# Attention with expert products on one core: splitting x^T a period earlier, decoding weights with the sign set in the shift, and a reordered fold

## The chip, the cores and the metric

The program runs on 1 core of one Trainium2 chip. The metric is device time in microseconds (us), median of the runs shown. Engines are named as in the profile: PE (TensorE; PEld is its weight loads), DVE (VectorE), ACT (ScalarE), POOL (GpSimd) and SP (SyncE, which issues all transfers).

## What is computed

```python
scores = scale * np.matmul(q, k.transpose(0, 1, 3, 2))      # 8 batches, 8 heads, 576 x 64
kth = np.partition(scores, -top_k, axis=-1)[..., -top_k:-top_k + 1]   # top_k = 32
scores = np.where(scores >= kth, scores, -1000000000.0)
...                                                         # softmax over the kept scores
attn_out = np.matmul(attn, v)
x = attn_out.transpose(0, 2, 1, 3).reshape(B * S, H * D)    # 4608 x 512
a = x @ w1; b = x @ w2                                      # 512 x 1024 each
h = a * b @ w3
out = h @ w_out                                             # 1024 x 512
```

The weights arrive as 64-bit numbers and are made into 32-bit ones on the chip.

## The kernel before, in words

**Slots.** Attention is cut into 144 slots, 18 to a batch (`SLOTS`): a slot is 128 queries for each of two heads. A slot passes through four stages, each in another turn of the loop `for p in range(-1, n_slots + 2)`, so that one turn (called a period here) works on four slots at once: `scores` of slot p+1 (PE, tile `st`, copied by ACT to `s`), `top32_steps` of slot p (DVE), `mask` and `exps` of slot p-1 (ACT, POOL and ACT again, tile `pab`), and `turn`, `values` and `store_x` of slot p-2 (PE tiles `tp` and `ro`, ACT copies `pts`, `pr`, `rec`, DVE writes `xt`, which is x^T).

**The search for the 32nd largest** on DVE opens with a fold of each row's 576 scores into 192 columns, four TENSOR_TENSOR over tile `w` (maximum and minimum of the first two thirds, then the third against that maximum), and goes on with four rounds of MAX8 (tile `top`) with MATCH_REPLACE between them. The first mask on POOL waits for the last operation of the fold that the finder hands out (`folded`).

**Expert products** of a batch are the generator `moe_steps`: one step is one PE matmul, 576 for a batch, and `fill(n)` takes n of them from the queue. `SHARE = 11, 11, 10` gives 32 to a period, so that one batch's products last exactly 18 periods, called a lap here. The steps are, for each half of the 576 rows, 192 matmuls into tiles `ab` (x times w1 and w2), and 96 into `eo`. All weights and x^T are held as a high and a low part. `split_x(h)` makes the parts of x^T, tiles `xf`: four copies on ACT and four subtractions on POOL for each half. Before the change the first `split_x(0)` is the first thing that the generator does when it is first asked for a step, so it stands in the same `fill` as the first `ab` matmuls. The queue gets a batch at the end of the period in which its last slot was stored.

**Weights** come in 80 units (16 of w_out, 48 of w3 and w1 mixed, two to one, 16 of w2). `warm()` starts one unit and moves every unit on its way one step: ACT makes `t` and a part of `y` from the raw `z`, DVE shifts `t` left by 3 into `z`, POOL adds, DVE puts the sign bit on, then ACT and POOL split it (`wh`, `wl`), or PE multiplies w3 by w_out into `pf`, which becomes `wf`. `warm()` is called four times a period, from the first period p = -1 on. Two units share one PSUM tile `t`, from the same three buffers as `pf`.

**Order.** `InOrder` (lines 38 to 53) keeps every engine's instructions in the order in which the program issues them, so that all of them carry line 48 in the profile and are told apart by their tiles. What `moe_steps` hands to `after` (copies out of PSUM, the split) goes on the list `put_off` and is issued at the head of the next `fill`. Places the change touches: `decode` (line 108), `top32_steps` (208), `moe_steps` with its `split_x` (325 to 393), `fill` and `warm` (446 to 475), and the loop (481 to 534).

Of the kernel before, what the change touches and what calls it, by code (L numbers as in the profile page):

```python
# [9 lines left out]
F32 = mybir.dt.float32  # L10
F32R = mybir.dt.float32r
I32 = mybir.dt.int32
# [7 lines left out]
NHP = H // 2  # L20
# [36 lines left out]
def attn_moe(ctx: ExitStack, tc: tile.TileContext, q, k, v, w1, w2, w3, w_out, out, flag, general):  # L57
# [50 lines left out]
    def decode(z, dst=None):  # L108

        if not bank:
            both = ps_m.tile([128, 512], F32, tag="mm", name="t")
            bank.extend((both[:, 256:], both[:, :256]))
        t = bank.pop()
        y = x_p.tile([128, 2 * HS], F32, tag="x", name="y")
        high = z[:, 1:512:2]
        low = z[:, :512].bitcast(U16)[:, 1:1024:4]  # L120
        r = y[:, 256:512].bitcast(I32)
        u = z[:, :256].bitcast(I32)
        act.activation(t, high, AF.Copy, scale=2.0**-112)
        act.activation(r, low, AF.Copy, scale=2.0**-13)
        yield
        ti = t.bitcast(I32)
        dve.tensor_scalar(u, ti, 3, None, op0=ALU.logical_shift_left)
        yield
        pool.tensor_tensor(r, u, r, op=ALU.add)
        yield  # L130
        dst = y[:, :256] if dst is None else dst
        dve.scalar_tensor_tensor(dst.bitcast(I32), ti, -(2**31), r, op0=ALU.bitwise_and, op1=ALU.bitwise_or)
        yield
        return dst

# [72 lines left out]
    def top32_steps(s, slot):  # L208

        w = att_p.tile([128, 2, S], F32, tag="w", name="w", bufs=1)
        top = tops[slot % len(tops)]
        one, two, three = slice(0, NG), slice(NG, 2 * NG), slice(2 * NG, S)
        dve.tensor_tensor(w[:, :, one], s[:, :, one], s[:, :, two], op=ALU.max)
        dve.tensor_tensor(w[:, :, two], s[:, :, one], s[:, :, two], op=ALU.min)
        dve.tensor_tensor(w[:, :, three], w[:, :, one], s[:, :, three], op=ALU.min)  # L220
        yield dve.tensor_tensor(w[:, :, one], w[:, :, one], s[:, :, three], op=ALU.max)
        for i in range(4):
            cut = slice(i * 8, (i + 1) * 8)
            for a in range(2):
                dve.max(top[:, a, cut], w[:, a, one] if i < 3 else w[:, a, :])
            if i < 3:
                for a in range(2):
                    dve.match_replace(w[:, a, one], top[:, a, cut], w[:, a, one], NEG)
                yield
# [35 lines left out]
    def exps(edge, pab, sums, a):  # L265
        p = pab[:, a, :]
        act.activation(p, p, AF.Exp, bias=edge[:, a, 0:1], scale=SCALE, accum_out=sums[:, a : a + 1])
# [54 lines left out]
            cols, n = (slice(512, 576), slice(j * 64, j * 64 + 64)) if t == 4 else (slice(t * 128, t * 128 + 128), slice(0, 128))  # L322
            dve.tensor_tensor(xt[:, cols], ov[:, n], rec[:, n], op=ALU.mult)

    def moe_steps(b, xt, after):

        xs = {}

        def split_x(h):
            lo, hi = HALVES[h]
            for x in xt:
                xf = x_p.tile([128, 2, HS], F32R, tag="x", name="xf")
                act.copy(xf[:, 0, :], x[:, lo:hi])
                pool.tensor_tensor(xf[:, 1, :], x[:, lo:hi], xf[:, 0, :].bitcast(F32), op=ALU.subtract)
                xs.setdefault(h, []).append(xf)

        def take_a(p, asb):
            act.copy(asb, p[:, :HS])
# [13 lines left out]
            else:  # L356
                sp.dma_start(outs[ds(b, 1)][:, es, lo:hi].rearrange("o p n -> (o p) n"), osb)

        split_x(0)
        for h, (lo, hi) in enumerate(HALVES):  # L360
            g = []
            for f in range(NFC):
                asb = o_p.tile([128, HS], F32, tag="o", name="asb")
                g.append(g_p.tile([128, 2, HS], F32R, tag="g", name="g"))
                for i in range(2):
                    p = ps_m.tile([128, 512], F32, tag="mm", name="ab")
                    for c in range(NCC):
                        for n, (w, x) in enumerate(((wh, 0), (wh, 1), (wl, 0))):
                            pe.matmul(
                                p[:, :HS], w[i][:, c * DF + f * 128 : c * DF + (f + 1) * 128], xs[h][c][:, x, :],  # L370
                                start=(c == 0 and n == 0), stop=(c == NCC - 1 and n == 2),
                            )
                            if (c, n) != (NCC - 1, 2):
                                yield
                    if i == 0:
                        after(lambda p=p, asb=asb: take_a(p, asb))
                    else:
                        after(lambda p=p, asb=asb, gf=g[f]: take_b(p, asb, gf))
                    yield
            if h == 0:  # L380
                after(lambda: split_x(1))
            for e in range(NEC):
                p = ps_m.tile([128, 512], F32, tag="mm", name="eo")
                for f in range(NFC):
                    for n, (i, j) in enumerate(((0, 0), (1, 0), (0, 1))):
                        pe.matmul(
                            p[:, :HS], wf[i][:, f * DM + e * 128 : f * DM + (e + 1) * 128], g[f][:, j, :],
                            start=(f == 0 and n == 0), stop=(f == NFC - 1 and n == 2),
                        )
                        if (f, n) != (NFC - 1, 2):  # L390
                            yield
                after(lambda p=p, e=e, lo=lo, hi=hi: take_o(p, e, lo, hi))
                yield
# [13 lines left out]
    if general:  # L407
# [3 lines left out]
        with tc.For_i(0, B, 1) as b:  # L411
            seen = small.tile([1, 1], I32, tag="seen", name="seen", bufs=1)
            nc.sync.dma_start(seen, flag[ds(b + 1, 1), :])
            with tc.If(nc.values_load(seen, min_val=0, max_val=1) > 0):
                kv, xs = {}, {}
                for hps, t in SLOTS:
# [12 lines left out]
                    tp, ro = turn(pab)  # L429
                    ov, rb = values([kv[hp][2] for hp in hps], t, *take_turned(tp, ro), sums, ro)  # L430
                    store_x([xs[hp] for hp in hps], t, ov, take_rb(rb))
                for _ in moe_steps(b, [xs[hp] for hp in range(NHP)], lambda f: f()):
                    pass
        return

# [1 line left out]
    kv, ss, edges, pabs, xts = {}, {}, {}, {}, {}  # L437
    queue = []

    put_off = []  # L440

    def evict():
        while put_off:
# [13 lines left out]
    def fetch_pair(u):  # L457
        if u < B * NHP:
            kv[u] = load_pair(u // NHP, u % NHP)
# [8 lines left out]

    def warm():

        if fetched:
            z, step = fetched.pop(0)
            going.append(step(z))
        going[:] = [unit for unit in going if next(unit, "end") != "end"]
        prefetch(5)
# [2 lines left out]
    prefetch(5)  # L478
    fetch_pair(1)
    n_slots = len(slots)  # L480
    for p in range(-1, n_slots + 2):
        i, j, m = p + 1, p - 1, p - 2
        if i < n_slots and slots[i][1] == 3:
            fetch_pair(slots[i][0][0] + 2)
        finder = top32_steps(ss[p], p) if 0 <= p < n_slots else iter(())
        if 0 <= m < n_slots:
            invert(pabs[m][1])
# [11 lines left out]
            pts, pr = take_turned(tp, ro)  # L499
        if 0 <= j < n_slots:  # L500
            exps(edges[j], *pabs[j], 0)
        fill(SHARE[1])
        next(finder, None)
        warm()
# [20 lines left out]
        if 0 <= m < n_slots:  # L525
            store_x([xts[u] for u in us], t, ov, rec)
            del ss[m], pabs[m], edges[m]
            if (m + 1) % NS == 0:
                b = m // NS
                queue.append(moe_steps(b, [xts[b * NHP + hp] for hp in range(NHP)], put_off.append))  # L530
        warm()
    while queue:
        fill(6)
    evict()

# [61 lines left out]
```

## Time and profile before

| | us |
|---|---|
| runs: median (lowest to highest of 3) | 1424.66 (1422.35 to 1425.04) |
| the profiled execution | 1422.13 |
| its span, first to last instruction | 1420.3 |
| busy in the span: PE, DVE, ACT, POOL | 1283.6, 1161.5, 980.1, 801.5 |
| first fold on DVE begins; first expert matmul begins | 11.51; 255.80 |
| last batch's products, with no attention left | from 1328.69 to 1409.09 |

The span has three parts: a start of some 20 periods in which weights are decoded beside attention, six laps in which a batch's products run beside the next batch's attention, and a tail with the last batch's products alone. Busy time of PE is modelled, so that 100% of a stretch means no gap that the profile knows of. PEclk is the clock granted to TensorE, as a share of 2.4 GHz.

### The profile page before, as it was taken

What the parts mean: (1) busy time and instruction counts of PE and PEld (TensorE: products, weight loads), DVE (VectorE), ACT (ScalarE), POOL (GpSimd) and SP (SyncE); (2) the same over time, 40 slices, a digit from 0 to 9 for tenths busy, and PEclk for the clock granted to TensorE, in tenths of its full rate; (3) what the DMA queues carried; (4) which work ended last, traced back from release to release, by engine and by line L of the source; (5) the groups of instructions that cost most, each with busy time, mean ns of one, the idle gap of its engine ahead of it and who ended that gap; (6) DMA issues with size and microseconds to landing.
All of it is one profiled execution on the core that took longest, in us unless ns stands there. A gap on an engine that the chain in (4) does not pass through costs nothing. (4 is left out here: it accounts for less than half of the span.)

```text
span 1420.3 us, 31033 instructions
## 1 busy us (share of the span) xinstructions
PE 1283.6 (90%) x11025; PEld 1106.5 (78%) x11025; DVE 1161.5 (82%) x4060; ACT 980.1 (69%) x2169; POOL 801.5 (56%) x1033
## 2 busy tenths in 40 slices
PE   2777765799989998999989998999899998999996
PEld 1433333698878897988979887889798997988996
DVE  7988889699979999799979997999979997999000
ACT  5766677577767777677767776777677776777321
POOL 4756568565646656465546564665646554656221
PEclk9999996799999999999999999999999999999999
DMA  6332331001010101001010101010100101000000
GB/s 223 94 119 70 108 118 57 30 12 65 12 46 30 47 30 47 20 21 57 20 56 12 65 12 46 31 46 30 47 20 20 57 21 56 12 18 2 18 18 20
DMA packets 34743, 64.99 MB, mean 46 GB/s; under 512 B 3860, under 2 KB 12052, under 8 KB 34580
## 3 DMA queue, kind: packets, MB, share of 16 engines
q1 hardware_dynamic: 34580, 62.93, 13.6%
q8 instruction: 88, 1.44, 0.4%
q14 instruction: 75, 0.61, 0.1%
HBM read 53.48 MB, written 9.44 MB: 44 GB/s over the span
## 5 line engine op out<-in xcount | busy, mean ns | idle before, releaser
L48 POOL TENSOR_TENSOR pab<-s,pab 128x576 f32<-128x576 f32 x288 | 402.7, 1419 | 235.4 <-DVE w L48 163.9
L48 PE MATMUL ab<-xf,wh 128*128 128x288 f32 x2048 | 445.9, 305 | 36.2 <-POOL xf L48 25.1
L48 DVE MAX8 top<-w 128x8 f32<-128x192 f32 (+1 forms) x1152 | 466.9, 446 | 2.4
L48 PEld LDWEIGHTS ab<-xf,wh 128*128 128x128 f32 x2048 | 341.3, 192 | 49.5 <-POOL xf L48 28.1
L48 PE MATMUL ab<-xf,wl 128*128 128x288 f32 x1024 | 313.2, 306 | 0.0
L48 ACT ACTIVATE pab<-s,edge 128x576 f32<-128x576 f32 x288 | 208.0, 771 | 144.3 <-POOL edge L48 144.3
L48 DVE MATCH_REPLACE8 w<-top,w 128x192 f32<-128x192 f32 x864 | 288.8, 341 | 0.0
L48 PE MATMUL st<-kt,qt 64*128 64x288 f32 (+1 forms) x1152 | 205.0, 443 | 47.0 <-ACT pts L48 32.4
L48 ACT ACTIVATE pab<-pab,edge 128x576 f32<-128x576 f32 x288 | 225.1, 782 | 21.1 <-POOL pab L48 20.7
L48 PE MATMUL eo<-g,wf 128*128 128x288 f32 x1536 | 228.6, 300 | 0.0
L48 PEld LDWEIGHTS eo<-g,wf 128*128 128x128 f32 x1536 | 208.4, 188 | 7.2 <-issue 7.2
L48 ACT COPY pts<-tp 128x1024 f32<-128x1024 f32 x144 | 145.4, 1010 | 88.0 <-PE tp L48 84.8
L48 PEld LDWEIGHTS ab<-xf,wl 128*128 128x128 f32 x1024 | 196.2, 192 | 4.8 <-issue 4.8
L48 PEld LDWEIGHTS st<-kt,qt 64*128 64x128 f32 (+1 forms) x1152 | 112.0, 191 | 100.8 <-ACT pts L48 43.3
L48 ACT COPY s<-st 128x576 f32<-128x576 f32 x288 | 181.7, 632 | 9.1 <-PE st L48 9.1
L48 POOL TENSOR_TENSOR g<-whole,g 128x288 fp32r<-128x288 f32 x128 | 102.7, 803 | 124.9 <-ACT g L48 94.5
L48 DVE TENSOR_TENSOR w<-w,s 128x384 f32<-128x384 f32 x288 | 161.3, 560 | 4.9
L48 PE MATMUL tp<-ident,pab 128*128 128x128 f32 x1152 | 155.7, 280 | 7.7 <-POOL y L48 7.7
L48 DVE TENSOR_TENSOR w<-s 128x384 f32<-128x384 f32 x288 | 159.6, 594 | 0.0
L48 PE MATMUL ro<-pts,vt 128*64 128x128 f32 (+1 forms) x2560 | 157.5, 267 | 0.0
L48 PEld LDWEIGHTS tp<-ident,pab 128*128 128x128 f32 x1152 | 139.6, 145 | 18.6 <-POOL y L48 8.5
L48 PEld LDWEIGHTS ro<-pts,vt 128*64 128x64 f32 x2560 | 138.2, 140 | 0.0
(49 smaller groups left out, 1293.6 us busy)
## 6 DMA issues: line engine op xcount, KB each, us to landing
z<-in_w SPq DMA_DIRECT2D x64, 256.0 KB, 2.7
vt<-in_v SPq DMA_DIRECT2D x32, 352.0 KB, 4.0
qt<-in_q SPq DMA_DIRECT2D x32, 320.0 KB, 3.0
kt<-in_k SPq DMA_DIRECT2D x32, 320.0 KB, 3.5
out_t<-osb SPq DMA_DIRECT2D x64, 144.0 KB, 1.7
z<-in_wo SPq DMA_DIRECT2D x16, 256.0 KB, 5.4
flag<-missed SPq DMA_DIRECT2D x1, 0.0 KB
seen<-flag SPq DMA_DIRECT2D x1, 0.0 KB
```

What stands on the lines that cost most here:

```text
L48: ins = fn(*args, **kw)
```

## The change

1. `decode`: DVE now does both of its operations in one step. It takes the sign bit of `t` into `z`, then shifts `t` and puts that sign on in one SCALAR_TENSOR_TENSOR into `y`; POOL's addition comes last and writes the result. An empty step keeps the number of steps.
2. `warm` is called five times a period (a new call before the second `fill`) and does nothing in the period p = -1.
3. The fold writes the maximum of the first two thirds into the third part of `w`; its last operation now writes that third part and no longer the part that the first MAX8 reads.
4. `split_x` leaves the generator. Two of the four parts are put off at the end of the period that stores the batch's last slot and two in the middle of the next; the generator is queued another period later, and the loop has one more turn. The second half's split is handed out as two pairs, behind the first and the second `eo` tile's begin.

```diff
@@ decode
-        dve.tensor_scalar(u, ti, 3, None, op0=ALU.logical_shift_left)
-        yield
-        pool.tensor_tensor(r, u, r, op=ALU.add)
+        dve.tensor_scalar(sign, ti, -(2**31), None, op0=ALU.bitwise_and)
+        dve.scalar_tensor_tensor(u, ti, 3, sign, op0=ALU.logical_shift_left, op1=ALU.bitwise_or)
         yield
         dst = y[:, :256] if dst is None else dst
-        dve.scalar_tensor_tensor(dst.bitcast(I32), ti, -(2**31), r, op0=ALU.bitwise_and, op1=ALU.bitwise_or)
+        pool.tensor_tensor(dst.bitcast(I32), u, r, op=ALU.add)
+        yield
         yield
@@ top32_steps
-        dve.tensor_tensor(w[:, :, one], s[:, :, one], s[:, :, two], op=ALU.max)
+        dve.tensor_tensor(w[:, :, three], s[:, :, one], s[:, :, two], op=ALU.max)
         dve.tensor_tensor(w[:, :, two], s[:, :, one], s[:, :, two], op=ALU.min)
-        dve.tensor_tensor(w[:, :, three], w[:, :, one], s[:, :, three], op=ALU.min)
-        yield dve.tensor_tensor(w[:, :, one], w[:, :, one], s[:, :, three], op=ALU.max)
+        dve.tensor_tensor(w[:, :, one], w[:, :, three], s[:, :, three], op=ALU.max)
+        yield dve.tensor_tensor(w[:, :, three], w[:, :, three], s[:, :, three], op=ALU.min)
@@ moe_steps
+    def split_x(xs, xt, h, pair):
+        lo, hi = HALVES[h]
+        for x in xt[2 * pair : 2 * pair + 2]:
...
-        split_x(0)
...
-            if h == 0:
-                after(lambda: split_x(1))
             for e in range(NEC):
+                if h == 0 and e < 2:
+                    after(lambda e=e: split_x(xs, xt, 1, e))
@@ warm
+        if p < 0:
+            return
@@ the loop
-    for p in range(-1, n_slots + 2):
+    for p in range(-1, n_slots + 3):
...
+        while starting:
+            queue.append(moe_steps(*starting.pop(0), put_off.append))
...
             exps(edges[j], *pabs[j], 0)
+        if ready and (m + 1) % NS:
+            put_off.append(lambda x=ready[0]: split_x(x[2], x[1], 0, 1))
+            starting.append(ready.pop(0))
+        warm()
         fill(SHARE[1])
...
             if (m + 1) % NS == 0:
-                b = m // NS
-                queue.append(moe_steps(b, [xts[b * NHP + hp] for hp in range(NHP)], put_off.append))
+                ready.append((m // NS, [xts[m // NS * NHP + hp] for hp in range(NHP)], ([], [])))
+                put_off.append(lambda x=ready[0]: split_x(x[2], x[1], 0, 0))
```

How the order of instructions moves, at the places that matter (buffer numbers are part of the names):

PE where one batch's products end and the next one's begin, before. `eo` is the old batch's last tile, `ab` the new batch's first, `tp` the turn of a slot's weights `pab`.

```order
L48 MATMUL eo_4379<-g_4049,wf0_100 128x288
L48 MATMUL ab_4501<-xf_4487,wh0_98 128x288 x2
L48 MATMUL ab_4501<-xf_4487,wl0_103 128x288
L48 MATMUL ab_4501<-xf_4490,wh0_98 128x288 x2
L48 MATMUL ab_4501<-xf_4490,wl0_103 128x288
L48 MATMUL ab_4501<-xf_4493,wh0_98 128x288 x2
L48 MATMUL ab_4501<-xf_4493,wl0_103 128x288
L48 MATMUL ab_4501<-xf_4496,wh0_98 128x288 x2
L48 MATMUL tp_4517<-ident_85,pab_4365 128x128 x8
```

The same place on PE in the changed program.

```order
L48 MATMUL eo_4462<-g_4120,wf0_100 128x288
L48 MATMUL ab_4573<-xf_4448,wh0_98 128x288 x2
L48 MATMUL ab_4573<-xf_4448,wl0_103 128x288
L48 MATMUL ab_4573<-xf_4451,wh0_98 128x288 x2
L48 MATMUL ab_4573<-xf_4451,wl0_103 128x288
L48 MATMUL ab_4573<-xf_4489,wh0_98 128x288 x2
L48 MATMUL ab_4573<-xf_4489,wl0_103 128x288
L48 MATMUL ab_4573<-xf_4492,wh0_98 128x288 x2
L48 MATMUL tp_4589<-ident_85,pab_4442 128x128 x8
```

The rows read alike; what moved is which slot's turn follows, and so what POOL does by then. POOL there, before:

```order
L48 TENSOR_TENSOR pab_4365<-s_4209,pab_4365 128x576 x2
L48 TENSOR_SCALAR sums_4366<-sums_4366 128x2
L48 TENSOR_TENSOR edge_4475<-top1_96,coef_90 128x4
L48 TENSOR_TENSOR over_93<-top1_96 128x2
L48 TENSOR_TENSOR pab_4478<-s_4317,pab_4478 128x576 x2
L48 TENSOR_TENSOR xf_4487<-xt_2451,xf_4487 128x288
L48 TENSOR_TENSOR xf_4490<-xt_2913,xf_4490 128x288
L48 TENSOR_TENSOR xf_4493<-xt_3505,xf_4493 128x288
L48 TENSOR_TENSOR xf_4496<-xt_3967,xf_4496 128x288
L48 TENSOR_SCALAR sums_4479<-sums_4479 128x2
L48 TENSOR_TENSOR edge_4602<-top2_97,coef_90 128x4
```

POOL, changed:

```order
L48 TENSOR_TENSOR pab_4326<-s_4171,pab_4326 128x576 x2
L48 TENSOR_SCALAR sums_4327<-sums_4327 128x2
L48 TENSOR_TENSOR edge_4439<-top1_96,coef_90 128x4
L48 TENSOR_TENSOR over_93<-top1_96 128x2
L48 TENSOR_TENSOR pab_4442<-s_4280,pab_4442 128x576 x2
L48 TENSOR_TENSOR xf_4448<-xt_2425,xf_4448 128x288
L48 TENSOR_TENSOR xf_4451<-xt_2868,xf_4451 128x288
L48 TENSOR_TENSOR xf_4489<-xt_3466,xf_4489 128x288
L48 TENSOR_TENSOR xf_4492<-xt_3922,xf_4492 128x288
L48 TENSOR_SCALAR sums_4443<-sums_4443 128x2
L48 TENSOR_TENSOR edge_4559<-top2_97,coef_90 128x4
L48 TENSOR_TENSOR over_93<-top2_97 128x2
```

Before, the four `xf` stand behind the masks of `pab_4478`, while PE's `ab` stand ahead of the turn of `pab_4365`, the slot one earlier: PE reaches them first. Now they stand behind the masks of `pab_4442`, and that is the very slot whose turn follows PE's `ab`: the split is ahead by one period.

DVE in a period of the start, from one fold to the next rounds, before (`t`, `z`, `y` and `wo` are decoding):

```order
L48 RECIPROCAL sums_324<-sums_324 128x2
L48 TENSOR_TENSOR w_412<-s_367 128x2x192 x2
L48 TENSOR_TENSOR w_412<-w_412,s_367 128x2x192 x2
L48 SCALAR_TENSOR_TENSOR wo_102<-t_314,y_356 128x256
L48 TENSOR_SCALAR z_286<-t_393 128x256
L48 MAX top0_95<-w_412 128x8 x2
L48 MATCH_REPLACE w_412<-top0_95,w_412 128x192 x2
L48 MAX top0_95<-w_412 128x8 x2
L48 MATCH_REPLACE w_412<-top0_95,w_412 128x192 x2
L48 SCALAR_TENSOR_TENSOR wo_102<-t_393,y_394 128x256
L48 TENSOR_SCALAR z_296<-t_420 128x256
L48 MAX top0_95<-w_412 128x8 x2
```

DVE, changed:

```order
L48 RECIPROCAL sums_309<-sums_309 128x2
L48 TENSOR_TENSOR w_406<-s_361 128x2x192 x2
L48 TENSOR_TENSOR w_406<-w_406,s_361 128x2x192 x2
L48 TENSOR_SCALAR z_281<-t_398 128x256
L48 SCALAR_TENSOR_TENSOR y_399<-t_398,z_281 128x256
L48 MAX top0_95<-w_406 128x8 x2
L48 MATCH_REPLACE w_406<-top0_95,w_406 128x192 x2
L48 TENSOR_SCALAR z_303<-t_398 128x256
L48 SCALAR_TENSOR_TENSOR y_414<-t_398,z_303 128x256
L48 MAX top0_95<-w_406 128x8 x2
L48 MATCH_REPLACE w_406<-top0_95,w_406 128x192 x2
L48 TENSOR_SCALAR z_340<-t_451 128x256
```

One unit's two DVE operations now stand side by side. Before, the one that sets the sign belongs to a unit two steps older and reads what POOL wrote.

ACT in such a period, before:

```order
L48 ACTIVATE pab_323<-s_199,edge_320 128x576 x2
L48 COPY pts_344<-tp_333 128x1024
L48 COPY pr_346<-ro_342 128x128
L48 ACTIVATE pab_323,sums_324<-pab_323,edge_320 128x576
L48 ACTIVATE t_314<-z_237 128x256
L48 ACTIVATE y_356<-z_237 128x256
L48 COPY s_367<-st_361 128x2x288
L48 ACTIVATE pab_323,sums_324<-pab_323,edge_320 128x576
L48 COPY s_367<-st_364 128x2x288
L48 COPY rec_384<-ro_342 128x128
```

ACT, changed:

```order
L48 ACTIVATE pab_308<-s_176,edge_305 128x576 x2
L48 COPY pts_329<-tp_318 128x1024
L48 COPY pr_331<-ro_327 128x128
L48 ACTIVATE pab_308,sums_309<-pab_308,edge_305 128x576
L48 ACTIVATE t_299<-z_236 128x256
L48 ACTIVATE y_337<-z_236 128x256
L48 ACTIVATE t_349<-z_248 128x256
L48 ACTIVATE y_350<-z_248 128x256
L48 COPY s_361<-st_355 128x2x288
L48 ACTIVATE pab_308,sums_309<-pab_308,edge_305 128x576
L48 COPY s_361<-st_358 128x2x288
L48 COPY rec_378<-ro_327 128x128
```

Two units (`t_299` and `t_349`) now stand behind the first exponential (the row with `sums`), where one stood.

## Rows read from the trace of the kernel before

**Rows 1.** The page's head: busy us, share of the span and instructions of each engine.

```profile
PE 1283.6 (90%) x11025; PEld 1106.5 (78%) x11025; DVE 1161.5 (82%) x4060; ACT 980.1 (69%) x2169; POOL 801.5 (56%) x1033
```

**Rows 2.** Busy time by stretches (start:end, length, then busy us and instructions of each engine, granted clock, DMA share, GB/s): the first and the last of the six laps (18 slots each), the other 17 slots of a lap without the slot in which a new batch's products begin, that slot alone, and a short slot without a product's DVE work.

```profile
391.75:545.67 153.92, 149.42 (x1364) 133.84 (x1363) 135.68 (x487) 113.52 (x246) 89.45 (x115) 0.99 0.11 36
...
1022.64:1176.26 153.62, 149.12 (x1364) 133.72 (x1364) 135.69 (x489) 113.53 (x247) 89.45 (x114) 0.99 0.11 37
...
422.45:561.54 139.09, 139.09 (x1291) 125.03 (x1290) 128.43 (x463) 106.35 (x230) 83.11 (x105) 1.00 0.10 32
...
407.61:422.45 14.84, 10.34 (x75) 8.82 (x75) 7.25 (x29) 7.17 (x18) 6.34 (x9) 0.89 0.18 63
...
1249.56:1257.01 7.45, 7.45 (x70) 6.40 (x69) 7.28 (x29) 5.57 (x13) 4.93 (x7) 1.00 0.12 43
```

**Rows 3.** Timeline where the second batch's products begin (start, us, engine, operation, out<-in, count, idle time before and what ended it).

```profile
406.92 1.59 PE L48 MATMUL eo<-g,wf 128*128 128x288 f32 x10
...
409.38 0.40 PE L48 MATMUL ab<-xf,wh 128*128 128x288 f32 x1 [0.86 <-ACT xf L48]
...
409.85 2.76 POOL L48 TENSOR_TENSOR pab<-s,pab 128x576 f32<-128x576 f32 x2 [2.63 <-DVE w L48]
...
412.57 3.06 POOL L48 TENSOR_TENSOR xf<-xt,xf 128x288 fp32r<-128x288 f32 x4
...
413.41 0.41 PE L48 MATMUL ab<-xf,wh 128*128 128x288 f32 x1 [3.64 <-POOL xf L48]
```

**Rows 4.** The stretch right behind that wait, columns as in rows 2.

```profile
413.70:417.10 3.40, 3.40 (x15) 3.15 (x15) 0.95 (x2) 0.00 (x0) 1.93 (x3) 0.50 0.00 0
```

**Rows 5.** The tail: the old batch's last ten matmuls in PE's timeline, right behind the last slot's values, and two pieces of the chain that ended last (start, us, what).

```profile
1326.23 1.59 PE L48 MATMUL eo<-g,wf 128*128 128x288 f32 x10
...
1370.70 25.60 PE ab L48 x192
...
1409.09 0.12 PE wp L48
```

**Rows 6.** Timeline of the first 12 us: the first scores on PE, the first score copies on ACT, the first fold on DVE.

```profile
4.62 2.29 PE L48 MATMUL st<-kt,qt 64*128 64x288 f32 x8 [4.62 <-DMA kt<-in_k]
...
9.33 1.16 ACT L48 COPY s<-st 128x576 f32<-128x576 f32 x2
...
11.51 1.55 DVE L48 TENSOR_TENSOR w<-s 128x384 f32<-128x384 f32 x2
```

**Rows 7.** Stretches of the start, columns as in rows 2: slots 7 to 15, the two slots in which w2 is decoded, and a stretch of low clock.

```profile
88.15:206.40 118.25, 90.02 (x502) 48.39 (x502) 99.78 (x315) 78.86 (x191) 70.64 (x94) 0.93 0.32 98
...
218.70:242.31 23.61, 13.22 (x82) 9.41 (x82) 21.99 (x69) 18.83 (x48) 19.60 (x27) 0.71 0.20 62
243.00:263.50 20.50, 9.03 (x47) 7.50 (x48) 16.43 (x54) 9.13 (x20) 15.16 (x19) 0.50 0.06 18
```

**Rows 8.** Groups of instructions in slots 7 to 15 (count, busy us, mean ns of one, idle us of the engine just before them and what ended it).

```profile
L48 DVE MAX8 top<-w 128x8 f32<-128x192 f32 (+1 forms) x72 | 29.2, 447 | 0.0
...
L48 DVE TENSOR_TENSOR w<-s 128x384 f32<-128x384 f32 x19 | 16.7, 916 | 0.0
L48 DVE TENSOR_SCALAR z<-t 128x256 int32<-128x256 int32 x36 | 15.1, 418 | 3.0 <-ACT y L48 3.0
L48 DVE SCALAR_TENSOR_TENSOR y<-t,y 128x256 int32<-128x256 int32 x36 | 15.1, 418 | 13.1 <-POOL y L48 13.1
...
L48 ACT ACTIVATE t<-z 128x256 f32<-128x256 f32 x36 | 14.9, 413 | 39.4 <-DVE wf L48 22.1 <-DVE y L48 13.7 <-DVE z L48 3.5
```

**Rows 9.** Groups over the whole span, columns as in rows 8.

```profile
L48 DVE MAX8 top<-w 128x8 f32<-128x192 f32 (+1 forms) x1152 | 466.9, 446 | 2.4
...
L48 DVE TENSOR_TENSOR w<-s 128x384 f32<-128x384 f32 x288 | 159.6, 594 | 0.0
...
L48 DVE TENSOR_TENSOR wf<-pf,wf 128x512 fp32r<-128x512 f32 x8 | 5.4, 680 | 0.0
```

**Rows 10.** Timeline of two folds: one of the start with what POOL does beside it, and one of a lap.

```profile
127.59 0.72 POOL L48 TENSOR_TENSOR y<-z,y 128x256 int32<-128x256 int32 x1
127.63 1.57 DVE L48 TENSOR_TENSOR w<-s 128x384 f32<-128x384 f32 x2
...
129.12 1.14 DVE L48 TENSOR_TENSOR w<-w,s 128x384 f32<-128x384 f32 x2
130.18 0.42 DVE L48 SCALAR_TENSOR_TENSOR y<-t,y 128x256 int32<-128x256 int32 x1
130.51 0.41 DVE L48 TENSOR_SCALAR z<-t 128x256 int32<-128x256 int32 x1
130.84 0.61 DVE L48 MAX8 top<-w 128x8 f32<-128x192 f32 x2
...
1161.33 1.14 DVE L48 TENSOR_TENSOR w<-w,s 128x384 f32<-128x384 f32 x2
1162.50 0.62 DVE L48 MAX8 top<-w 128x8 f32<-128x192 f32 x2
```

**Rows 11.** PE's timeline at the end of the values of the period in which the first products begin, and two groups of four `pf` matmuls (one w3 unit), at full and at low clock.

```profile
267.50 0.39 PE L48 MATMUL ro<-pr,vt 128*64 128x128 f32 x4
...
66.06 1.98 PE L48 MATMUL pf<-wo,y 128*128 128x512 f32 x4 [1.10 <-DVE y L48]
...
130.65 3.52 PE L48 MATMUL pf<-wo,y 128*128 128x512 f32 x4 [4.33 <-DVE y L48]
```

More of the change, by code (lines that the diff above doesn't have):

```diff
@@ L120, in decode @@
         low = z[:, :512].bitcast(U16)[:, 1:1024:4]
-        r = y[:, 256:512].bitcast(I32)
-        u = z[:, :256].bitcast(I32)
+        u, r = y[:, :256].bitcast(I32), y[:, 256:512].bitcast(I32)
+        sign = z[:, :256].bitcast(I32)
         act.activation(t, high, AF.Copy, scale=2.0**-112)
@@ L323, in store_x, with moe_steps @@
             dve.tensor_tensor(xt[:, cols], ov[:, n], rec[:, n], op=ALU.mult)
[L325 to L339, printed above, removed]
+    def split_x(xs, xt, h, pair):
+        lo, hi = HALVES[h]
+        for x in xt[2 * pair : 2 * pair + 2]:
+            xf = x_p.tile([128, 2, HS], F32R, tag="x", name="xf")
+            act.copy(xf[:, 0, :], x[:, lo:hi])
+            pool.tensor_tensor(xf[:, 1, :], x[:, lo:hi], xf[:, 0, :].bitcast(F32), op=ALU.subtract)
+            xs[h].append(xf)
+    def moe_steps(b, xt, xs, after):
         def take_a(p, asb):
@@ L431, in attn_moe @@
                     store_x([xs[hp] for hp in hps], t, ov, take_rb(rb))
-                for _ in moe_steps(b, [xs[hp] for hp in range(NHP)], lambda f: f()):
+                xt, parts = [xs[hp] for hp in range(NHP)], ([], [])
+                for pair in range(2):
+                    split_x(parts, xt, 0, pair)
+                for _ in moe_steps(b, xt, parts, lambda f: f()):
                     pass
@@ L438, in attn_moe @@
     queue = []
-    put_off = []
+    put_off, ready, starting = [], [], []
     def evict():
@@ L528, in attn_moe @@
             if (m + 1) % NS == 0:
-                b = m // NS
-                queue.append(moe_steps(b, [xts[b * NHP + hp] for hp in range(NHP)], put_off.append))
+                ready.append((m // NS, [xts[m // NS * NHP + hp] for hp in range(NHP)], ([], [])))
+                put_off.append(lambda x=ready[0]: split_x(x[2], x[1], 0, 0))
         warm()
-    while queue:
+    while starting or queue:
+        while starting:
+            queue.append(moe_steps(*starting.pop(0), put_off.append))
         fill(6)
```

## The prediction

> **What bounds the kernel now.** I read the page's head first: PE is the busiest engine at 90% of the span, DVE follows with 82% [rows 1]. These are means over a start, six laps and a tail, so the next view is busy time by stretches. In a lap, 17 of 18 slots (139.09 us) have PE busy for the whole of the stretch at full clock, while DVE has 128.43, ACT 106.35 and POOL 83.11 us of work in it [rows 2]. Modelled ends could hide waits in that. But in the tail, where nothing else runs, 192 `ab` matmuls take 25.60 us, 0.133 us each [rows 5], and in the short slot of the lap 26 products leave 7.45 - 26 x 0.133 = 4.0 us for the slot's attention, so PE has no hidden reserve: it is the bound of the laps.
>
> The exception is the slot in which a new batch's products begin. It takes 14.84 us, with PE busy for 10.34 and a granted clock of 0.89 [rows 2]. The timeline says why: the old batch ends at 408.3, the first `ab` waits 0.86 us for ACT's copy of x^T, the second 3.64 us for POOL's subtraction, which stands behind two masks (2.76 us) that themselves wait for DVE's fold [rows 3]. Behind the wait TensorE's clock is at 0.50, its 1.2 GHz level, for 3.40 us [rows 4]. This comes once a lap.
>
> The start is another regime: slots 7 to 15 take 118.25 us, 13.1 each, with DVE busy for 99.78, PE 90.02, ACT 78.86 and POOL 70.64 [rows 7]. DVE sets it, and loses some 19 us to waits for POOL's and ACT's parts of decoding; ACT waits 22.1 us for `wf` on DVE, since `t` and `pf` share buffers [rows 8].
>
> **The split a period earlier.** Nothing is added: the same 4 copies and 4 subtractions for each half. In the changed order POOL gets to the new batch's parts behind the masks of the period before PE asks for them. PE's first demand today comes 412.57 + 0.77 - 409.38 = 4.0 us too early for the first part [rows 3], and a period is 139.09 / 17 = 8.18 us, so the parts are 4 us early. PE then runs the lap at its own pace: 18 x 8.18 = 147.3 instead of 153.62 to 153.92 [rows 2], 6.5 us less, and **39 us in six laps**. Both the idle time (4.5) and the slow clock behind it (about 1.9) are in this. Bounds: nothing, if another engine needs the time; not more than 6.5, since PE's own work does not shrink. I take all of it, because DVE's 135.7 us for a lap is 92% of 147.3 [rows 2]. The moved subtractions stand ahead of `sums` on POOL, for which DVE's reciprocal and next fold wait; POOL has 6.34 us of work in that slot [rows 2] against 8.18, so I cost this at nothing, and 0.8 us a lap (one subtraction) if the cover is gone. ACT's two copies ahead of `pts` are 0.7 us on an engine with 7.17 us of work there. The second half's split in pairs only thins POOL out.
>
> **The tail.** Today ten `eo` begin at 1326.23, so the last batch could start at 1327.57 and its 576 products need 76.8 us: 1404.4. They end at 1409.09 [rows 5]. In the changed program 42 products (5.6 us) stand between the last values and the new batch, in which its split is made (store 0.3, two copies 0.7, subtractions 3.1). **4.6 us go.**
>
> **One period later.** The laps begin in period 21 instead of 20. Before the values of period 20 end at 267.8 [rows 11], 22 products were done; now none is: **2.9 us more** behind that point.
>
> **The start.** What counts is when the values of period 20 end. The first fold waits for score copies that stand behind two decoded units on ACT, 9.33 us, while the scores are there at 6.9 [rows 6]; with nothing decoded in period -1 it starts at about 7.6 instead of 11.51. Then 16 periods with five units instead of 20 with four:
> - DVE's attention, 7.2 us (the short slot without product work [rows 2]).
> - Five units. Two operations start 0.33 us apart [rows 10]. The second now waits for the first. No decode row shows such a wait; the fold does: where the fold's last operations are followed by one that needs them, MAX8 begins 1.17 us behind them, where by one that doesn't, 1.06 [rows 10]. So 0.11 us a unit, between nothing and 0.2: 5 x (0.33 + 0.33 + 0.11) = 3.9 us.
> - `wf`, eight of 0.6 us [rows 9] over 16 periods: 0.3.
> - The fold beside POOL: 916 ns in the start against 594 overall [rows 8, 9], twice: 0.6.
> - Waits. Those for POOL's addition (13.1 us in nine slots [rows 8]) end, because that addition is now last, and ACT's for `wf` should: `t` is free two steps sooner. What is late next is ACT: two units now stand behind the first exponential, which waits for the mask, and DVE's third unit of a period needs the first of these. I put 0.8 us; bounds 0 and the 2.1 a slot of today (19 us in nine).
>
> That is 12.8 a period, 205 us for 16, less 2 for the first ones, which have no masks or stores. Period 16 drains the pipeline; POOL, with 19.60 us in the two slots of four w2 units [rows 7], sets some 9.3. Periods 17 to 20 have attention alone: 7.3 us by DVE, but at 0.50 clock PE would need 8 of its own, so 8.0. Values of period 20 then end at 7.6 + 203 + 9.3 + 32 - 0.7 = 251, and some 2.5 us are lost while products begin at the low level, as they did in the stretch of 0.50 [rows 7]. 267.8 to 253.7: **14 us less**. Bounds: with no waits, no stretched fold and no own wait 45 us less; at 14.5 a period 14 more than today.
>
> **The fold** has the same four operations. Its last one is no longer what MAX8 needs: 0.11 us of DVE a slot, off the path in the laps, and in the start a decode operation follows anyway. Nothing, and nothing is lost if DVE should matter.
>
> Here a page speaks against the rows. A wait on the operation just before costs 0.11 us [rows 10]. The Trainium skill, VectorE: DVE Perf Modes, section The DRAIN you can't avoid, says that a Vector operation starts only when the one before has drained, and that a semaphore between them costs nothing extra. By that rule the sum would be 80 x 0.11 = 9 us lower, by the rows it stands. The trace disagrees with it.
>
> A second rule concerns the fifth unit. POOL's addition at 127.59 lies beside two fold operations of 1.57 us, 1.2 by the overall mean [rows 9, 10]; MAX8, with one input, has 447 ns in the start and 446 overall [rows 8, 9]. The Trainium skill, SBUF — State Buffer, section SBUF: two separate sides, has a Vector operation with two SBUF inputs and a GpSimd operation that reads SBUF shut each other out. The trace agrees. By that rule a second addition beside the fold would cost up to 0.7 us a period, 11 us in all; the added calls lie beside MAX8, so I count none.
>
> **Sum**: -39 - 4.6 + 2.9 - 14 = -54.7 against the profiled execution: span 1420.3 to 1365.6, and with the 1.8 us around it 1367.4. The median of the runs shown is 2.5 above that execution; I say 1368.
>
> **The rivals.**
> 1. *The laps keep their length*, because DVE takes up what PE frees. For it: in the short slot DVE is busy 7.28 of 7.45 us [rows 2]. Against: over 17 slots it is 128.4 of 139.1. Only start, tail and shift remain: -15.7, some 1407. 7%.
> 2. *The start does not get shorter*: ACT's order or POOL (23.61 us for two w2 slots with 19.60 of POOL's work [rows 7]) makes a five-unit period 14.5 us. -39 - 4.6 + 2.9 + 14 = -27, some 1396. 8%.
> 3. *The split is still late*: parts made earlier, but PE waits for the second pair. It does so if POOL reaches that pair more than 4 us later than reckoned; half of the wait left costs 20 us: 1388. 3%.
> 4. *Slower*: TensorE stays at 1.2 GHz while w3 is folded. A w3 unit took 1.98 us, and 3.52 mostly at low clock [rows 11]; 3.3 of them with 8 us of attention make PE's period 20 us over 9.6 periods, 69 more than reckoned: 1437. It decides once the values of period 20 end after 308 (267.8 + 39 + 4.6 - 2.9). Against: PE's idle time there came from waiting for `y`, which is now ready two steps sooner; clock 0.93 [rows 7]. 3%.
> 5. *The own wait is free*: 80 units at 0.66 instead of 0.77 us: 9 less, 1359. The folds speak against it [rows 10]. 3%.
> 6. *A second addition beside each fold*: 16 x 0.7 = 11 more, 1379. The order puts the added calls elsewhere, but POOL may run late. 4%.
>
> **Numbers.** Forecast 72%. The range goes from 1350 (a start without the waits and stretches I put in, half of the way to its bound) to 1397, which takes in rivals 2, 3, 5 and 6 and leaves out 1 and 4. A difference of 0.2% (2.8 us) is about what a measurement can tell. Every case but the fourth is faster: 0.95, with 0.04 for the fourth and for rival 1 and 2 together with a still longer start, and 0.01 for a balance.
>
> **What the next profile would show.** Right: no idle time of PE before `ab` with `xf` as its releaser; no 0.50 stretch between 270 and the end; laps of 147 to 148 us; first fold near 7.6; decoding over by slot 17; values of period 20 near 251. Wrong, step by step: laps of 150 or more with PE idle behind `pts` or `st` (rival 1), idle DVE before `z` with ACT's `y` as releaser, periods above 14 (rival 2), PE's clock at 0.5 in slots 4 to 13 (rival 4).

## The result, and the profile after

The changed kernel takes 1368.38 us (median of four runs, 1368.20 to 1368.85), the kernel before 1423.86 beside it: a ratio of 0.9611, 95% interval 0.9595 to 0.9628. A second series gave 1369.00 (1368.69 to 1369.26), ratio 0.9615, 0.9602 to 0.9628. The forecast was 1368, in a range of 1350 to 1397. The profiled execution has a span of 1367.1 us.

The page of the changed kernel: the engines' head, the granted clock by slices, the chain's shares by engine (the chain of work that ended last), and two of the groups with the idle time before them in the last column.

```profile
PE 1269.8 (93%) x11025; PEld 1101.1 (81%) x11025; DVE 1156.8 (85%) x4060; ACT 981.7 (72%) x2169; POOL 784.6 (57%) x1033
...
PEclk6889977999999999999999999999999999999998
...
PE 79%; DVE 12%; ACT 5%; issue 2%; POOL 1%; DMA 0%; DVEq 0%; SPq 0%; POOLq 0%; ACTq 0%
...
L48 PE MATMUL ab<-xf,wh 128*128 128x288 f32 x2048 | 432.5, 299 | 0.0
...
L48 PE MATMUL st<-kt,qt 64*128 64x288 f32 (+1 forms) x1152 | 206.0, 445 | 60.6 <-ACT pts L48 50.9
```

The `ab` group stood like this on the page of the kernel before:

```profile
L48 PE MATMUL ab<-xf,wh 128*128 128x288 f32 x2048 | 445.9, 305 | 36.2 <-POOL xf L48 25.1
```

PE never idles before `ab` any more, and no slice between the start and the last one has a clock below 9. Most of the idle time that PE has left lies before scores. By stretches (columns as in [rows 2]): the first and the last of the six laps, then periods 0 to 15 (five units each), period 16, and periods 17 to 19; a period is counted from one fold to the next.

```profile
393.44:540.44 147.00, 147.00 (x1364) 132.40 (x1363) 134.86 (x488) 113.71 (x247) 87.39 (x114) 1.00 0.11 37
981.47:1128.47 147.00, 147.00 (x1364) 132.38 (x1363) 134.89 (x489) 113.70 (x247) 87.12 (x114) 1.00 0.11 37
7.91:216.42 208.51, 142.42 (x777) 82.91 (x775) 187.72 (x582) 146.64 (x359) 135.97 (x181) 0.81 0.41 121
216.42:226.91 10.49, 5.91 (x37) 4.71 (x37) 9.11 (x29) 7.18 (x17) 9.13 (x13) 0.53 0.20 63
226.91:248.24 21.33, 14.74 (x123) 9.99 (x122) 21.23 (x80) 16.30 (x33) 11.06 (x16) 0.91 0.01 2
```

A lap is 147.00 us with the same 1364 matmuls as before [rows 2], busy from end to end at clock 1.00. The timeline where the second batch begins answers to [rows 3]:

```profile
398.44 3.08 POOL L48 TENSOR_TENSOR xf<-xt,xf 128x288 fp32r<-128x288 f32 x4
...
400.82 1.60 PE L48 MATMUL eo<-g,wf 128*128 128x288 f32 x10
402.25 0.42 PE L48 MATMUL ab<-xf,wh 128*128 128x288 f32 x2
```

The four subtractions (two pairs; here one row) end at 401.52, and the first `ab` follows the old batch's last `eo` without a gap. The end of the start, in PE's timeline (the last values of period 20 and the first product), answers to [rows 11]; three pieces of the chain of the tail answer to [rows 5].

```profile
254.78 0.39 PE L48 MATMUL ro<-pr,vt 128*64 128x128 f32 x4
255.09 0.53 PE L48 MATMUL ab<-xf,wh 128*128 128x288 f32 x2
```

```profile
1271.60 5.80 PE eo L48 x42
1277.40 25.60 PE ab L48 x192
...
1354.19 0.12 PE wp L48
```

The values of period 20 end at 255.17 instead of 267.89 [rows 11], 12.7 us less; `wp` comes at 1354.19 instead of 1409.09 [rows 5], 54.9 less. So 42.2 us were won behind that point, and 12.7 ahead of it. The span shrank by less, 53.2 us: from `wp` to its end it is 11.2 us before and 12.9 after. The last section comes back to this.

### The profile page after: what moved, and what is told of

It is laid out like the page before. It is cut to its first block, busy times and chain, and to the rows that moved or that the text cites. A ratio compares the mean times of both kernels' runs of the same rounds, so it can differ in the third digit from the quotient of the medians.

```text
span 1367.1 us, 31053 instructions
## 1 busy us (share of the span) xinstructions
PE 1269.8 (93%) x11025; PEld 1101.1 (81%) x11025; DVE 1156.8 (85%) x4060; ACT 981.7 (72%) x2169; POOL 784.6 (57%) x1033
## 4 chain that ended last, share of the span: by engine, by line
PE 79%; DVE 12%; ACT 5%; issue 2%; POOL 1%; DMA 0%; DVEq 0%; SPq 0%; POOLq 0%; ACTq 0%
PE ab L48 30%; PE eo L48 15%; PE ro L48 14%; PE st L48 11%; PE tp L48 8%; DVE w L48 5%; DVE top L48 3%; ACT pab L48 2%; DVE y L48 2%; DVE z L48 1%; ACT pts L48 1%; PE pf L48 1%; ACT y L48 1%; POOL wl L48 0%; ACT t L48 0%
## 5 line engine op out<-in xcount | busy, mean ns | idle before, releaser
L48 PE MATMUL ab<-xf,wh 128*128 128x288 f32 x2048 | 432.5, 299 | 0.0
L48 PEld LDWEIGHTS ab<-xf,wh 128*128 128x128 f32 x2048 | 332.8, 188 | 8.3 <-issue 7.4
L48 PE MATMUL ab<-xf,wl 128*128 128x288 f32 x1024 | 309.8, 303 | 0.0
L48 PEld LDWEIGHTS ab<-xf,wl 128*128 128x128 f32 x1024 | 192.2, 188 | 4.8 <-issue 4.8
L48 PE MATMUL ro<-pts,vt 128*64 128x128 f32 (+1 forms) x2560 | 163.3, 273 | 0.0
L48 DVE TENSOR_TENSOR w<-s 128x384 f32<-128x384 f32 x288 | 155.9, 581 | 7.9 <-ACT s L48 7.9
L48 PEld LDWEIGHTS tp<-ident,pab 128*128 128x128 f32 x1152 | 135.8, 143 | 24.7 <-POOL wo L48 13.2
L48 PEld LDWEIGHTS ro<-pts,vt 128*64 128x64 f32 x2560 | 143.7, 144 | 0.0
```

Source lines behind the costliest of these rows:

```text
L48: ins = fn(*args, **kw)
```

## Experiments: which part pays

All times are medians; the kernel before ran beside each series at 1423.11 to 1423.73.

**The split alone.** The changed kernel with decoding and fold as before, and these edits to the calls of `warm()`:

```diff
 def warm():
-        if p < 0:
-            return
...
             starting.append(ready.pop(0))
-        warm()
         fill(SHARE[1])
```

> The change with only the split of x^T made ahead and the added period; decoding with its three operations, four units a period from period -1 on, and the fold as before. Theory (laps become PE's own, the start is a separate gain): slots 0 to 19 stay as before (slot 20 begins at 252.8), slot 20 loses its stall, so the values of period 20 end near 260, and the laps are 147.0 us: 13 to 14 us are lost of the gain of the changed kernel's start of 12.7 less what slot 20 keeps, so 1368.4 + 4.5 = 1373. If the parts of the change were simply additive terms of the forecast (-39 - 4.6 + 2.9): 1383. Rival (laps keep their length because another engine takes what PE frees): 1407 with laps above 152.

Measured: 1373.65, ratio 0.9654 (0.9639 to 0.9668). Stretches: periods 0 to 19, period 20, a lap.

```profile
11.81:253.23 241.42, 159.03 (x939) 91.64 (x935) 215.20 (x684) 167.74 (x402) 157.43 (x205) 0.90 0.33 102
253.23:262.25 9.02, 4.94 (x38) 4.06 (x37) 7.91 (x27) 6.59 (x15) 7.68 (x11) 0.81 0.07 25
399.49:546.49 147.00, 147.00 (x1364) 132.34 (x1363) 135.47 (x488) 113.69 (x247) 88.90 (x114) 1.00 0.11 37
```

The laps are those of the changed kernel. The split alone is worth 49.5 us, not the 40.7 that its terms in the forecast sum to: period 20 also falls, from 15.72 us before to 9.02, since the first batch had the same wait as the others.

**Decoding and the fifth call alone**, on the kernel before (the hunks in `decode` and `warm()`, and the new call of `warm()`).

> The kernel before with only the new decoding and five units a period, none in period -1; the split of x^T and the fold as before. Theory: the laps stay at 153.6 to 153.9 us with PE waiting for xf; slots 0 to 19 end at 248.2 instead of 252.8, slot 20 with its wait takes 15 to 16 us: 1423.9 - 4.6 = 1419. The forecast's term for the start taken alone would be -14: 1410. Rival (the start gains nothing): 1424.

Measured: 1418.94, ratio 0.9971 (0.9959 to 0.9983), a gain of 4.2 us. Periods 0 to 19, period 20 and a lap:

```profile
7.79:248.80 241.01, 161.29 (x928) 95.60 (x926) 218.49 (x688) 170.38 (x408) 156.13 (x208) 0.82 0.37 108
248.80:264.62 15.82, 10.62 (x68) 9.44 (x69) 7.25 (x28) 7.22 (x17) 6.92 (x11) 0.63 0.08 24
403.72:558.03 154.31, 149.81 (x1364) 134.42 (x1364) 135.70 (x488) 113.44 (x247) 89.45 (x114) 0.98 0.11 34
```

The start ends 4 us earlier and what lies behind it is as before [rows 2]. 49.5 and 4.2 make 53.7; the whole change gained 55.5 us, and 54.7 in the second series. The fold is in neither part, so the parts add to within 1 to 2 us.

**The old order of the fold**, in the changed kernel (the hunk in `top32_steps` undone).

> The changed kernel with the fold's four operations in their old order. Forecast: the reorder is worth nothing on the path: 1368.4, within 1.4 us. Rival (its 0.11 us a slot is on DVE's path in the 16 decoding periods): 16 x 0.11 = 1.8 us slower, 1370.2; on the path in all 144 slots: 15 us slower, 1383.

Measured: 1370.06 (1369.03 to 1370.83), ratio 0.9627 (0.9614 to 0.9640), 1.1 to 1.7 us above the two medians of the changed kernel; the intervals overlap, so the times alone do not show a difference. The fold's second pair and MAX8 in period 17, first in this kernel, then in the changed one:

```profile
227.99 1.14 DVE L48 TENSOR_TENSOR w<-w,s 128x384 f32<-128x384 f32 x2
229.16 0.62 DVE L48 MAX8 top<-w 128x8 f32<-128x192 f32 x2
```

```profile
227.87 1.14 DVE L48 TENSOR_TENSOR w<-w,s 128x384 f32<-128x384 f32 x2
228.93 0.61 DVE L48 MAX8 top<-w 128x8 f32<-128x192 f32 x2
```

1.17 us against 1.06: 0.11 per fold, as reckoned from [rows 10]. But the 16 decoding periods are hardly longer for it: 208.87 us against 208.51. What shows is 0.12 us in each of the short periods in which DVE has little but attention (17, 18, 19, 21, 23); by the folds of the two traces the kernel is 0.75 us behind in period 38, and as much in period 143. So the traces give the new order some 0.8 us, and not in the place that the rival named.

**The old decoding**, with five calls a period (the hunks in `decode` undone).

> The changed kernel with the old decoding of three steps (DVE, POOL, DVE), still five units a period. Theory (the new order takes DVE's wait for POOL away, 13 us in nine slots of before, and pays about 0.15 us a unit for the own wait): the periods grow from 13.0 to 13.5 to 14.3 us, 8 to 20 us over 16 periods, so 1376 to 1388, DVE waiting before y for POOL. Rival (the new decoding only moves the wait from DVE to ACT): the periods stay at 13.0, 1368; with the own wait saved (80 x 0.15 = 12 us) even 1357.

Measured: 1383.67, ratio 0.9722 (0.9707 to 0.9737), 15 us slower than the changed kernel. Periods 0 to 15, and DVE's longest wait in the window 68 to 204 us (us in total, times, longest):

```profile
7.82:232.09 224.27, 147.14 (x777) 80.89 (x775) 181.40 (x580) 147.45 (x361) 140.31 (x181) 0.80 0.36 112
```

```profile
DVE y L48 <- POOL y L48: 15.8, 7, 2.7
```

224.27 against 208.51 for the same units, with 6.3 us less work on DVE: the new decoding pays by ending waits, with DVE's for POOL before `y` as the largest group of them (in the window 68 to 189.6 us of the changed kernel none is left), not by less work.

**Four units a period, new decoding**: the diff shown for the split, alone.

> The changed kernel with four units a period from period -1 on, the new decoding kept. It stands against the run with only the split (same count, old decoding: 1373.7, slot 20 begins at 253.2) and the changed kernel (five units, 1368.4 to 1369.0, slot 20 at 248.2). If the new decoding is worth as much at four units as at five (there 15 us): slot 20 begins near 240 and 1361. If it pays only where ACT and DVE are crowded by the fifth unit: the periods stay at 12.3 to 12.5, slot 20 begins near 251 to 253 and 1371 to 1374. If its own wait makes it dearer at four: 255 or later, 1376.

Measured: 1367.07 (1365.15 to 1367.76), ratio 0.9602 (0.9588 to 0.9617). Periods 0 to 19:

```profile
12.27:243.88 231.61, 159.74 (x933) 97.07 (x931) 218.94 (x682) 168.90 (x402) 155.55 (x205) 0.87 0.35 105
```

A middle result: period 20 begins at 243.9, 9.4 us earlier than with the old decoding at four (253.2), and 4.4 earlier than with five (248.2). A period of four takes 11.6 us, one of five 13.0. So **the fifth call is worth nothing**: what it saves in periods it pays back in their length. By the times, four and five units cannot be told apart (the intervals overlap).

## Experiments: why five units take 13 us

In the changed kernel the periods of the start alternate: 12.5 and 14.3, 11.8 and 14.6 us. Groups in the window 68 to 189.6 us (count, busy us, mean ns, idle before and its releaser):

```profile
L48 DVE SCALAR_TENSOR_TENSOR y<-t,z 128x256 int32<-128x256 int32 x45 | 19.1, 425 | 3.6
L48 DVE TENSOR_SCALAR z<-t 128x256 int32<-128x256 int32 x45 | 18.8, 417 | 6.4 <-ACT y L48 6.3
L48 ACT ACTIVATE t<-z 128x256 f32<-128x256 f32 x45 | 18.5, 411 | 34.9 <-DVE y L48 34.9
L48 DVE TENSOR_TENSOR w<-s 128x384 f32<-128x384 f32 x19 | 15.0, 829 | 0.0
L48 DVE TENSOR_TENSOR wf<-pf,wf 128x512 fp32r<-128x512 f32 x8 | 5.5, 683 | 2.5 <-ACT wf L48 2.5
```

And a long period (timeline, all engines):

```profile
123.51 0.41 DVE L48 TENSOR_SCALAR z<-t 128x256 int32<-128x256 int32 x1
123.95 0.42 DVE L48 SCALAR_TENSOR_TENSOR y<-t,z 128x256 int32<-128x256 int32 x1
...
124.41 0.40 ACT L48 ACTIVATE t<-z 128x256 f32<-128x256 f32 x1 [2.92 <-DVE y L48]
...
125.07 1.42 ACT L48 ACTIVATE pab<-s,edge 128x576 f32<-128x576 f32 x2
...
125.90 2.77 POOL L48 TENSOR_TENSOR pab<-s,pab 128x576 f32<-128x576 f32 x2 [3.46 <-DVE z L48]
...
127.45 0.78 ACT L48 ACTIVATE pab<-pab,edge 128x576 f32<-128x576 f32 x1
...
128.22 0.39 ACT L48 ACTIVATE t<-z 128x256 f32<-128x256 f32 x1
...
129.00 0.42 DVE L48 TENSOR_SCALAR z<-t 128x256 int32<-128x256 int32 x1 [1.42 <-ACT y L48]
```

ACT's `t` waits for DVE's `y`, by the program that of the unit in the other half of its buffer; behind it on ACT stand the first half of the mask (`pab<-s,edge`) and, by POOL's mask, the exponential; behind that the next unit's `t` and its part of `y`, for which DVE waits 1.42 us. POOL's masks are put down to DVE's `z`, which ended just then; but a mask reads `pab`, whose first half ACT finished at about the same time, so that this step of the chain is inferred. Two theories followed: move the first call behind the masks, or part the neighbours' halves.

```diff
         folded = next(finder, None)
-        warm()
         if 0 <= j < n_slots:
...
                 mask(ss[j], edges[j], pabs[j][0], a, folded if a == 0 else None)
+        warm()
```

> The changed kernel with the first decoding call of a period issued behind the masks instead of ahead of them. Theory (in the changed kernel POOL's masks and ACT's Relu stand behind a decoding step that itself waits, and POOL's addition lies beside the fold): the fold's operations go from 829 ns back to about 600 in the start, the first exponential comes earlier, and the periods fall from 13.0 to between 12.0 and 12.5: 8 to 16 us less, 1352 to 1360. Rival (the decoding step only waits elsewhere, DVE's own work of 12.0 and its third unit decide): 1365 to 1370. If the call then falls together with the next one on POOL and holds up exponentials' turning: up to 1380.

```diff
-            both = ps_m.tile([128, 512], F32, tag="mm", name="t")
-            bank.extend((both[:, 256:], both[:, :256]))
+            two = [ps_m.tile([128, 512], F32, tag="mm", name="t") for _ in range(2)]
+            bank.extend((two[1][:, 256:], two[0][:, 256:], two[1][:, :256], two[0][:, :256]))
```

> The changed kernel with the two halves of a buffer of t given to units that are two calls apart instead of neighbours. Theory (ACT's t waits for y's shift on DVE, of the unit before in the same buffer, 34.9 us in nine periods, and this is what makes every second period 2 us longer): the periods become even, 12.0 to 12.6 us, 6 to 16 us less: 1352 to 1362. Rival (the three buffers that t shares with pf and the products' sums are the limit, since two are now half used for longer): pf waits for a buffer, the periods grow to 13.5 or more, 1376 or more.

> Both edits together: the first call behind the masks, and the halves of a buffer of t two calls apart. If the two waits are separate, their gains add: 1340 to 1355. If they are one chain (POOL's masks late because ACT's t is late), the better one of the two alone. DVE's own work of 12.0 us a period is the floor: 16 x 1.0 = 16 us less, 1352, or 9 us lower if the fold too goes back to 600 ns.

> The changed kernel once more, on the same chip as the three that follow, as their base: 1368.4, within 1.4 us.

Measured in one series: the changed kernel 1369.00, the call behind the masks 1369.24 (ratio to before 0.9622, 0.9609 to 0.9635), the halves parted 1372.48 (0.9639, 0.9626 to 0.9652), both 1375.59 (0.9664, 0.9651 to 0.9677). No theory of a gain held. Yet most of the waits that were aimed at did go. ACT's waits for DVE's `y` before `t`, 34.9 us in this window, were 18.3 with the call moved and these with the halves parted, so the shared buffer did cause most of them:

```profile
ACT t L48 <- DVE y L48: 7.3, 8, 1.7
```

With the call moved (groups and PE's waits, same window):

```profile
L48 DVE TENSOR_TENSOR w<-s 128x384 f32<-128x384 f32 x16 | 8.1, 550 | 0.0
```

```profile
PE pf L48 <- POOL y L48: 19.3, 6, 4.2
```

The fold's operations fell from 829 to 550 ns, and seven of the first 16 periods took 10.0 to 12.1 us, where four did in the changed kernel. But PE now waited 19.3 us, in front of the `pf` matmuls that fold a w3 unit, for POOL's addition; in the changed kernel that wait is 0.5. One such place (timeline; PE and ACT):

```profile
165.21 3.78 PE L48 MATMUL pf<-wo,y 128*128 128x512 f32 x4 [4.25 <-POOL y L48]
...
168.78 2.97 PE L48 MATMUL st<-kt,qt 128*128 128x288 f32 x8
...
170.82 0.64 ACT L48 COPY s<-st 128x576 f32<-128x576 f32 x1 [3.62 <-PE st L48]
```

In PE's order the scores stand behind `pf` and begin only as it ends, at 168.78, and ACT's copy of them waits 3.62 us. The four `pf` behind the wait take 3.78 us, where others took 1.98 at full clock and 3.52 mostly at low clock [rows 11]. This period (the one from 159.48) took 16.3 us. With the halves parted the place is the same and the releaser another:

```profile
PE pf L48 <- DVE wf L48: 27.2, 4, 7.7
```

There `pf` waits, by the program, for one of the three buffers it shares with `t`. With both edits both waits are there: 17.0 us for POOL's `y` and 11.2 for DVE's `wf`. So the moved call freed DVE, ACT and POOL, and, it seems, PE's order took it back. That can be tested: let PE come to `pf` one call later, in `load_w3`.

```diff
         y = yield from decode(z)
+        yield
         if i == 0:
```

> The kernel with the first call of a period behind the masks (1369.2), and besides the matmul that folds a w3 unit into pf one call later in PE's order. Theory (with the call moved, the fold's operations fell to 550 ns and the periods without a w3 fold to 11.0 to 12.0 us, but PE waited 19.3 us in nine slots for y of POOL's addition in front of pf, and the scores stood behind it): that wait goes, the long periods fall from 14 to 16 to about 12.3, slot 20 begins at 232 to 240 and the whole takes 1352 to 1360. Rival (the three buffers that pf, t and the sums of the products share, or ACT's order, set the long periods): pf is held one call longer and nothing is gained, 1369 or more.

> The changed kernel with only the matmul of a w3 unit into pf one call later (the first decoding call stays ahead of the masks): the missing cell beside the runs with the call moved alone (1369.2) and with both (1349.5). Theory: in the changed kernel PE waits only 1.9 us in nine slots in front of pf, so there is nothing to win alone, and the fold stays at 829 ns: 1367 to 1370. Rival (the later matmul is the whole gain of the pair, through the buffers' order): 1350 to 1356.

Measured: the later matmul alone 1368.83 (0.9618, 0.9605 to 0.9632); together with the moved call **1349.50** (1348.90 to 1350.71), ratio 0.9484 (0.9471 to 0.9497). Each edit alone is worth nothing, both together 19.5 us, against the changed kernel's 1369.00, and more than was expected (1352 to 1360). Periods 0 to 15, the fold and PE's wait for POOL's addition in the same window as above, and `wp` in the chain:

```profile
7.53:196.76 189.23, 138.33 (x777) 79.54 (x775) 178.72 (x581) 146.78 (x359) 123.75 (x181) 0.83 0.46 135
```

```profile
L48 DVE TENSOR_TENSOR w<-s 128x384 f32<-128x384 f32 x20 | 10.2, 548 | 0.0
```

```profile
PE pf L48 <- POOL y L48: 0.5, 1, 0.5
```

```profile
1334.37 0.12 PE wp L48
```

In front of `pf` PE waits 8.7 us in this window for all engines together, where with the call moved alone it was 23.5. DVE is busy for 178.7 of 189.2 us, where it was for 187.7 of 208.5: 9 us less work (the fold beside nothing) and 10 less waiting. `wp` comes 19.8 us earlier than in the changed kernel, which is what these 16 periods (19.3) and the earlier first fold (0.4) make: what the start gains reaches the end undiminished.

> The kernel with both edits (1349.5) with four units a period from period -1 on. Theory (with five, the slots now run at DVE's own work of 11.5 us, and a fifth unit costs about 0.8 to 1.0 us a period while it saves four periods of 11.5 - 7.1 less its share): four gives slots of 10.8 to 11.2 for twenty periods, slot 20 at 12.3 + 18 x 11.0 + 10.0 + 10.0 = 230 to 236 against 228.4: 1350 to 1357. Rival (as in the changed kernel, four is the better count): slot 20 before 227, 1346 to 1349.

Measured with four units: 1351.20 (1349.40 to 1352.91), ratio 0.9490 (0.9477 to 0.9502), the first fold at 12.08 and period 20 at 231.29 against 228.44. The two ratios' intervals overlap: with both edits, too, four and five units cannot be told apart by the times.

## Why the prediction was right, and where it was not

**The laps**: right. 147.00 us against 147.3, no wait of PE before `ab`, no dip of the clock, and no other engine took the time; the signs that the forecast named for them are there. Its margin was too generous: the parts were to be 4 us early. In the second batch the four subtractions end 3.2, 2.8, 2.4 and 2.1 us ahead of the matmul that reads each, and so within 0.1 us in the next five; in the first batch, which starts at the end of the decoding, it is 1.3, 1.0, 0.6 and 0.2. It was enough, but in the first batch rival 3 (PE waits for the second pair) was missed by 0.2 us.

**Behind period 20**, laps, tail and the added period were to give 40.7 us and gave 42.2. The second half of the split and POOL's later `sums` cost nothing that shows.

**The start**: -12.7 us for -14, by errors that offset one another. First fold 7.91 for 7.6 (+0.3); 16 periods 208.5 for 203 (+5.5); period 16 10.5 for 9.3 (+1.2); periods 17 to 20 shorter by 3.0 than the 31.3 reckoned, because PE was not on the low clock there (0.91) and DVE's 7.1 us set them; and the 2.5 us for a slow clock at the first products did not come, since the clock was at 1.00 from the first `ab` (1.00 in the stretch 255.09 to 258.00). Sum +1.5.

**The total** met the forecast partly by luck. These 1.5 us stand against 1.5 more behind period 20, so that `wp` comes 54.9 us earlier, for 54.7 reckoned. That the end behind `wp` grew by 1.7 us was in no term. And the step from 1367.4, the time forecast for the profiled execution, to 1368 added 0.6, where the text itself puts the median of the kernel before 2.5 above its profiled execution.

**Inside the periods** two terms were too small, and they about make up the 5.5. DVE's waits for other engines in the 16 periods, put at 0.8 us each, are 14.6 us in all, 0.9 each (11.1 before `z` and 2.5 before `wf`, both for ACT, 1.0 in four short ones): 1.8 more. The mechanism that was named (units ahead of the exponential on ACT) is there; what was not seen is the shared buffer of `t`, and that PE's `pf` takes over when these waits go. DVE's own wait was put at 0.11 us a unit: in the changed kernel the shift begins 0.44 or 0.52 us behind the mask operation in the long period above, and 0.49 on average over the 80 units, where independent ones were 0.33 apart [rows 10]. That is 0.16 a unit, so some 4 us more; the fold's two orders give 0.11. The Trainium skill, VectorE: DVE Perf Modes, section The DRAIN you can't avoid, says that such a semaphore costs nothing extra; these traces disagree.

**The other rivals.** Rival 6, a second addition beside each fold, did not come: the fold's operations take 829 ns with five units and 817 with four. The first addition costs what the sum held for it, 0.6 us: 829 against 550 ns, twice a period. The Trainium skill, SBUF — State Buffer, section SBUF: two separate sides, has these operations shut each other out; the two traces agree. Rival 4's sign was there in part: the clock in periods 0 to 15 was 0.81, against 0.93 in [rows 7]. It did not set the time: a second profile of the changed kernel had 0.86 there, and the periods took 208.7 us as well.

**What the forecast credited to the wrong part.** It put 14 us to the decoding and the fifth call and 40.7 to the split. By the single runs the split is worth 49.5 and the others 4.2, mostly because the stall of period 20 (6.7 us) stood in the start's term. Within those 4.2 the decoding gives and the fifth call takes nothing or a little: 1373.65 to 1367.07 at four units (the fold's order in it), then 1368.4 to 1369.0 with five. The forecast never asked what four units would take with the new decoding. The fold, put at nothing, is worth some 0.8 us by the traces.

## What to carry to other kernels

Where a bound engine waits once per batch for prepared operands, prepare them a stage earlier and price it at the wait plus the slow clock behind it; then look whether the first batch has the same wait, since that gain hides in another term. Before raising the rate of a side stream, time the old rate with the cheaper step. And when an edit removes a wait and the time stays, look at what now stands in order ahead of the critical work: two edits that are worth nothing alone can be worth 19.5 us together.

## What the runs showed of the hardware

A GpSimd addition of 0.7 us beside two VectorE operations with two SBUF inputs lengthened these from 550 to 829 ns on average, while MAX8, with one input, stayed at 444 to 447 ns in the same windows. VectorE operations that need the result of the one just before began later than independent ones: MAX8 1.17 us behind the fold's last pair where it reads what that wrote, 1.06 where it does not.

From `wp` to the end of the span it is 10.7 to 11.2 us in the three profiles with the old decoding (the kernel before, the split alone, the old decoding with five calls) and 12.7 to 13.6 us in the eleven with the new one. So the new decoding seems to cost some 2 us behind the last matmul, which the stretches of the start do not show; no run was made to find the cause.
